# Three moves in a transformer block: a modulation's weights after two steps instead of none, a projection's order, and the first loads' queues

## The chip, the cores and the metric

The kernel runs on one core of one Trainium2 chip. The metric is the device time of one execution in microseconds (us), the median of several runs. A core has five engines that run their own instruction streams: TensorE (PE: matrix products), VectorE (DVE), ScalarE (ACT), GpSimd (POOL) and SyncE (SP, which here only issues transfers). Transfers run on 16 DMA engines, and an instruction stream that issues one goes on to its next instruction, unless the transfer itself must first wait for something: then everything behind it in that stream waits too.

## The reference

A transformer block with adaptive layer norm, all in 32-bit floats: S = 2048 rows, D = 576 columns, 32 heads of 18.

```
mod = (silu(c) @ w_mod).reshape(1, 6, 1, 576)      # c: 1 x 576, w_mod: 576 x 3456
sa, ca, ga, sb, cb, gb = the six of mod
h = layernorm(x) * (1 + ca) + sa
x = x + ga * attention(h, wqkv, wo)                # softmax over 2048 keys, scale 18 ** -0.5
h = layernorm(x) * (1 + cb) + sb
x = x + gb * ((sigmoid(h @ w_gate) * (h @ w_up)) @ w_down)   # inner width 4608
```

## The kernel before

**Start.** The rows of x come in four chunks of 512, each as four tiles of 128 rows (`rows_in`, L421). A chunk is normalized (`normalized`: statistics L215 and L216 on DVE, then the inverse square root from POOL's power L229 and two refinement rounds L232 to L235 on DVE, then L240), turned by PE (`ln_transpose`, L249), scaled by the modulation on ACT into `hT` (with DVE's L268 and L274 for a low-order part), and projected to queries and keys (`project_qk`, L348) and values (L405). `project_qk` makes the query half and the key half one after the other, or with `together` side by side, tile by tile. The first two of the six modulations (1.18 MB per 256 rows of `w_mod`, 2.65 MB in all) are computed here: `load_mod` L125 and matmuls L173. POOL also takes the difference of chunk 0's and chunk 1's keys (`key_differences`, L379 to L384, tiles `kd_d` and `kd_e`), which the maxima use later. In this stage PE, DVE and ACT run in the order in which the code is written, and POOL and SP in an order that a scheduler makes.

**Attention.** 32 units follow, each two heads for 1024 queries, in 16 steps (`kt`) of 128 keys. In a step PE computes scores (L1091), ACT takes their exponentials (L1095), PE multiplies by the values (L676); beside it PE computes scores once more (L571) for a unit ahead, of which DVE takes maxima (L577, L582). When a unit's maxima are complete, L589 on DVE gathers them, and `spread` turns them, splits them (L607 on DVE) and writes them by four transfers (L611, tile `mrows`) into the query tile of the next unit, whose scores L1091 can't be computed before. A unit's end is `outputs`: its sums of exponentials go out to memory and come back turned (L700, L701), DVE takes their reciprocal (L709), which goes out and comes back as a broadcast (L711, L713), POOL multiplies by it (L717). PE, ACT and SP run in the written order here; DVE and POOL in the scheduler's.

**The other four modulations.** In units 1 and 3 `load_mod` (L129 twice with 1.18 MB each, L130 with 0.29 MB) fetches 2.65 MB of `w_mod` each time, `weigh` multiplies them by silu(c) row by row and adds them up on POOL (L143, L146), and in units 2 and 4 `modulate` sums over the partitions on PE (L173), turns the result and hands it out (gates by L204, L205). What the first of these matmuls waits for is the end of `weigh`.

```
if kt == 0 and 0 < u < UNITS - 2:
    load_heads(u + 2)
if u in (1, 3):
    if kt == 0:
        ...
        mods = load_mod(a, b, 1 + u // 2)
        ...
        weighed = weigh(mods)
```

Of the kernel before, what the change touches and what calls it, by code (L numbers as in the profile page):

```python
# [23 lines left out]
P = 128  # L24
S = 2048
D = 576
# [6 lines left out]
DM = 512  # L33
# [52 lines left out]
def tile_block(ctx, tc, x_in, wqkv, wo, w_gate, w_up, w_down, c_in, w_mod, out):  # L86
    nc = tc.nc
    x_rows = x_in[0].rearrange("(t p) d -> p t d", p=P)
# [24 lines left out]
    def bank():  # L113

        turns["bank"] += 1
        return ps[turns["bank"] % 7].tile([P, 512], F32, name=f"s{turns['bank'] % 7}")
# [172 lines left out]
    def terms(wh, wl, cols, tiles=5):  # L289
        got = []  # L290
        for t in range(4):
            got += [(wh[:, t, cols], t), (wh[:, t, cols], 4 + t), (wl[:, t, cols], t)]
        if tiles == 5:
            got += [(wh[:, 4, cols], 8), (wl[:, 4, cols], 8)]
        return got
# [40 lines left out]
    def project_qk(both, ahead=None, together=False):  # L336

        pl = stages[0].tile([P, 2, 1024], F32R, name="pl")
        accs = [bank() for _ in both] if together else []
        all_ = [terms(wh, wl, slice(0, P)) for (_, wh, wl), _ in both]  # L340
        places = [(i, n) for i in range(len(both)) for n in range(len(all_[i]))]
        if together:
            places.sort(key=lambda at: min(at[1] // 3, 4))
        for i, n in places:
            if i == len(accs):
                accs.append(bank())
            (w, t), ch = all_[i][n], both[i][1]
            nc.tensor.matmul(  # L348
                accs[i], w, hT[:, t, ch * 512 : (ch + 1) * 512],
                start=n == 0, stop=n == len(all_[i]) - 1, skip_group_check=together,  # L350
            )
            if n < len(all_[i]) - 1:
                continue
            acc = accs[i]
            if ahead:
                ahead()
            hi, lo = (pl[:, l, i * 512 : (i + 1) * 512] for l in range(2))
            nc.scalar.copy(hi, acc)
            nc.vector.tensor_sub(lo, acc, hi.bitcast(F32))
        for i, ((parts, wh, wl), ch) in enumerate(both):  # L360
            p0 = 0
            for col, n in parts:
                which, f0 = col // D, col % D
                nc.sync.dma_start(
                    (qd, kd)[which][:, f0 : f0 + n, ch * 512 : (ch + 1) * 512]
                    .rearrange("l f n -> f l n").bitcast(F32),
                    pl[p0 : p0 + n, :, i * 512 : (i + 1) * 512].bitcast(F32),
                )
                p0 += n
        return pl  # L370
# [45 lines left out]
    with tc.tile_pool(name="ln", bufs=2) as ln:  # L416
        def rows_in(ch):
            xs = []
            for j in range(4):
                xt = ln.tile([P, 640], F32, name="x", bufs=8)  # L420
                nc.sync.dma_start(xt[:, :D], x_rows[:, ch * 4 + j, :])  # L421
                xs.append(xt)
            return xs

        def normalized(xs, first=None):
            mv = ln.tile([P, 4, 2], F32, name="mv")
            rs = ln.tile([P, 4], F32, name="rs")
            for j, xt in enumerate(xs):
                if first is not None and j == 3:
                    turned_c = po.tile([P, 512], F32, name="o")[:, 0:5]  # L430
                    nc.vector.tensor_mul(first[0:5, 256:384], first[0:5, 0:P], first[0:5, P:256])
                    nc.tensor.transpose(turned_c, first[0:5, 256:384], ident[0:5, 0:5])
                ln_stats(ln, xt[:, :D], mv[:, j, :])
            if first is not None:
                nc.vector.tensor_copy(sc, turned_c)
                nc.vector.tensor_copy(
                    first[:, 384:544].rearrange("p (t c) -> p t c", c=32), sc.unsqueeze(2).to_broadcast([P, 5, 32])
                )
            ln_scales(ln, mv, rs)
            for j, xt in enumerate(xs):  # L440
                ln_apply(xt, xt[:, :D], mv[:, j, 0:1], rs[:, j : j + 1])
            return xs

        order = ExitStack()
        order.enter_context(
            tc.manual_schedule(engines={mybir.EngineType.PE, mybir.EngineType.DVE, mybir.EngineType.Activation})
        )
        wv0 = ExitStack()
        wvp = wv0.enter_context(tc.tile_pool(name="wv0", bufs=1))
        with tc.tile_pool(name="wmp", bufs=1, side="right") as wmp:  # L450
            row = wmp.tile([P, 544], F32, name="mrow")
            nc.vector.memset(row[0:5, 0:P], 0.0)
            nc.scalar.dma_start(row[0:4, 0:P], c_in[0, 0:DM].rearrange("(t p) -> t p", p=P))
            nc.scalar.dma_start(row[4:5, 0:64], c_in[0:1, DM:D])
            rows_now = rows_in(0)
            nc.scalar.activation(row[0:5, P:256], row[0:5, 0:P], AF.Sigmoid)
            warm = early.tile([P, 1], F32, name="warm")
            nc.scalar.activation(warm[0:5], row[0:5, P : P + 1], AF.Exp)
            wm = wmp.tile([P, 5, 2 * D], F32, name="wm")
            wm = load_mod(wm[:, 0:4, :], wm[:, 4, :], 0)  # L460
            zs = normalized(rows_now, row)
            wts, splits = zip(*(load_qk([(o, P)], True) for o in (0, D)))
            rows_now = rows_in(1)
            wv, split_v = load_v(wvp, 0, True)
            turned = []

            def turn_some(*which):
                return lambda: turned.extend(ln_turned(zs, i) for i in which)

            for _ in modulate(  # L470
                row, wm, QUARTERS, [(mcol[:, 1, :], 0.0), (mcol[:, 0, :], 1.0)],
                (turn_some(0, 1), turn_some(2), turn_some(3, 4)),
            ):
                pass
        stages.append(right.enter_context(tc.tile_pool(name="stage", bufs=2, side="right")))
        ones = vaug[:, :, 0 : H * VW].rearrange("p t (h e) -> p t h e", e=VW)
        for t in range(NT):
            nc.gpsimd.memset(ones[:, t, :, DH:VW], 1.0)
        nc.gpsimd.memset(vaug[:, :, H * VW :], 1.0)
        for split in splits:  # L480
            split()
        ln_transpose(ln, None, hT, 0, turned)
        split_v()
        with tc.tile_pool(name="kdp", bufs=1) as kdp:
            zs = normalized(rows_now)
            pls = []
            for ch in range(NCH):
                pls.append(project_qk([(wt, ch) for wt in wts], together=not ch))
                project_v(wv, 0, 4 * ch)
                if not ch:  # L490
                    project_v(wv, 0, 2)
                if ch + 1 < NCH:
                    ln_transpose(ln, zs, hT, (ch + 1) * 512)
                if ch + 2 < NCH:
                    zs = normalized(rows_in(ch + 2))
                if ch:
                    project_v(wv, 0, 4 * ch + 2)
                if ch == 2:
                    key_differences(kdp, pls[0][:, :, 512:1024], pls[1][:, :, 512:1024], 0, P, 0)
        order.close()  # L500
        wv0.close()
# [128 lines left out]
    with tc.tile_pool(name="wv1", bufs=1) as wvp:  # L630
# [3 lines left out]
        for i, parts in enumerate(tiles):  # L634
            wt = load_qk(parts)
# [416 lines left out]
    for u in range(UNITS):  # L1052
        half, p = divmod(u, H // 2)
        qs, ks = heads(u)
        for kt in range(NT):
# [41 lines left out]
            if kt == 0 and 0 < u < UNITS - 2:  # L1097
                load_heads(u + 2)
            if u in (1, 3):
                if kt == 0:  # L1100
                    a = big.tile([P, 8, 640], F32, name="big")
                    a = a.rearrange("p a b -> p (a b)")[:, 0 : 8 * D].rearrange("p (t c) -> p t c", t=4)
                    b = slots.tile([P, 2560], F32, name="w0")[:, 0 : 2 * D]
                    mods = load_mod(a, b, 1 + u // 2)
                    row = slots.tile([P, 2560], F32, name="w1")[:, 0:544]
                    weighed = weigh(mods)
                elif kt >= 5:
                    next(weighed, None)
            elif u in (2, 4) and kt in (2, 4):
                takes = [(ga_b, None), (mcol2[:, 1, :], 0.0)] if u == 2 else [(mcol2[:, 0, :], 1.0), (gb_b, None)]  # L1110
                if kt == 2:
                    weighed = modulate(row, mods[:1], HALVES, takes)
                next(weighed, None)
            if 4 * NT + 8 <= step < FROM0 and step % 4 != 3:
# [541 lines left out]
    for n, (hf, b, k) in enumerate(seq):  # L1656
# [13 lines left out]
        if sevens:  # L1670
# [28 lines left out]
            for v in range(2):  # L1699
# [3 lines left out]
                if v == 0 and f is not None:  # L1703
                    t = gate(st, to)
# [155 lines left out]
```

## Time and profile before

| | us |
|---|---|
| median of 3 runs | 2765.57 (2763.77 to 2766.93) |
| profiled execution | 2765.01 |
| its span, first to last instruction | 2763.2 |
| TensorE busy in the span | 2738.9 |
| start to first exponential of unit 0 | 233.35 |
| first exponential of units 1, 2, 3, 4, 5 | 273.31, 311.25, 350.81, 389.39, 433.38 |

The 1.8 us between the profiled execution and its span lie before the first and after the last instruction. The starts of the units are those of the first L1095 of each; units that run without other work take 37.7 us.

### The profile page before, as it was taken

How to read it: one execution, taken by the hardware profiler on the slowest of the kernel's cores; microseconds unless marked ns; L12 is line 12 of the kernel's file. 1: busy time of each engine (PE TensorE's matmuls, PEld its weight loads, DVE VectorE, ACT ScalarE, POOL GpSimd, SP SyncE). 2: the span in 40 equal slices, each digit the busy share in tenths (PEclk: the TensorE clock that was granted, in tenths of full speed). 3: DMA queues.
4: the chain of work that ended last, by engine and by line, in shares of the span. 5: the costliest groups of instructions: out<-in, count | busy, mean ns of one | idle time of the engine just before them, and what ended most of it. 6: DMA issues, size and time to landing. Idle time of an engine off the chain costs nothing.

```text
span 2763.2 us, 50773 instructions
## 1 busy us (share of the span) xinstructions
PE 2738.9 (99%) x18430; PEld 1829.9 (66%) x18430; DVE 2281.0 (83%) x4318; ACT 1601.7 (58%) x3038; POOL 832.5 (30%) x1077
## 2 busy tenths in 40 slices
PE   7999999999999999999999999999999999999999
PEld 6975444444444544444444888888888888888888
DVE  7278989999999889999883888878888677777777
ACT  4316989999999789999988323333333222222221
POOL 2122327888853213760133222222221100000000
PEclk9999999999999999999999999999999999999999
DMA  5342334555553121432137766667767956666663
GB/s 175 124 156 97 88 105 157 194 189 197 185 172 108 52 57 52 146 100 75 54 116 246 255 234 227 242 224 271 278 244 295 329 198 198 202 195 202 198 198 118
DMA packets 184812, 480.03 MB, mean 174 GB/s; under 512 B 29734, under 2 KB 93742, under 8 KB 174450
## 3 DMA queue, kind: packets, MB, share of 16 engines
q1 hardware_dynamic: 163640, 377.39, 41.1%
q0 software_dynamic: 20912, 99.41, 10.2%
q8 instruction: 145, 2.38, 0.4%
q14 instruction: 105, 0.86, 0.1%
q10 hardware_dynamic: 10, 0.00, 0.0%
HBM read 294.80 MB, written 181.38 MB: 172 GB/s over the span
## 4 chain that ended last, share of the span: by engine, by line
PE 95%; DVE 2%; DMA 1%; issue 1%; SPq 0%; ACT 0%; POOL 0%; DVEq 0%; ACTq 0%; POOLq 0%
PE x L1247 28%; PE o L676 20%; PE s L1091 13%; PE s L571 11%; PE d L1397 8%; PE d L1329 6%; PE s L348 4%; PE s L820 2%; PE s L405 1%; DMA wq_raw<-in_A_wqkv_dram 1%; PE d L1595 0%; DVE Oa L1401 0%; PE s L931 0%; PE s L602 0%; DMA wv_raw<-in_A_wqkv_dram 0%
## 5 line engine op out<-in xcount | busy, mean ns | idle before, releaser
L1095 ACT ACTIVATE p<-s 128x512 f32<-128x512 f32 x2048 | 1070.0, 624 | 88.1 <-PE s L1091 58.5
L577 DVE TENSOR_REDUCE mx<-s 128x1 f32<-128x512 f32 x1568 | 1001.1, 684 | 104.4 <-PE s L571 76.9
L676 PE MATMUL o<-p,vaug 128*32 128x256 f32 (+1 forms) x5848 | 596.3, 478 | 0.2 <-ACT oT L694 0.2
L571 PE MATMUL s<-k,q 54*128 54x512 f32 x1920 | 551.7, 437 | 0.0
L1091 PE MATMUL s<-q,k 56*128 56x512 f32 x1920 | 532.2, 440 | 1.9 <-DMA q<-mrows 1.9
L1091 PEld LDWEIGHTS s<-q,k 56*128 56x128 f32 x1920 | 251.9, 185 | 254.3 <-DVE mx L577 73.7
L571 PEld LDWEIGHTS s<-k,q 54*128 54x128 f32 x1920 | 278.0, 185 | 211.2 <-DVE mx L582 66.2
L1247 PE MATMUL x<-k,w 128*128 128x512 f32 x1512 | 368.0, 391 | 0.0
L1247 PEld LDWEIGHTS x<-k,w 128*128 128x128 f32 x1512 | 277.2, 188 | 53.5 <-issue 1.7
L676 PEld LDWEIGHTS o<-p,vaug 128*32 128x32 f32 x5848 | 116.9, 108 | 206.1 <-issue 189.7
L1397 PE MATMUL d<-wd,hh 128*128 128x288 f32 x1248 | 249.8, 295 | 0.3 <-DVE Oa L1401 0.3
L1247 PE MATMUL x<-w,w 128*128 128x512 f32 x1008 | 244.5, 391 | 0.0
L1247 PE MATMUL x<-big,w 128*128 128x512 f32 x1008 | 244.4, 391 | 0.0
L1247 PEld LDWEIGHTS x<-big,w 128*128 128x128 f32 x1008 | 185.3, 188 | 35.5 <-DVE u L1761 0.2
L1247 PEld LDWEIGHTS x<-w,w 128*128 128x128 f32 x1008 | 184.4, 188 | 33.9
L1397 PEld LDWEIGHTS d<-wd,hh 128*128 128x128 f32 x1248 | 202.1, 188 | 4.3 <-DVE Oa L1401 0.8
L1397 PE MATMUL d<-wd,hl 128*128 128x288 f32 x624 | 184.3, 295 | 0.0
L1401 DVE TENSOR_TENSOR Oa<-Oa,d 128x288 f32<-128x288 f32 x312 | 136.5, 453 | 53.3 <-PE d L1397 49.3
L582 DVE CUSTOM_DVE_ANT_0 over<-s,over 128x512 f32<-128x512 f32 x240 | 163.9, 683 | 1.3 <-PE s L1091 0.3
L580 ACT ACTIVATE over<-s 128x512 f32<-128x512 f32 x240 | 147.6, 615 | 3.1 <-PE s L571 1.1
L1201 POOL TENSOR_TENSOR S<-raw 128x384 f32<-128x384 f32 x72 | 74.5, 1052 | 232.3 <-DVE w L1238 150.1
L1256 ACT ACTIVATE sg<-x 128x512 f32<-128x512 f32 x36 | 21.5, 598 | 205.2 <-PE x L1247 205.2
(273 smaller groups left out, 3807.6 us busy)
## 6 DMA issues: line engine op xcount, KB each, us to landing
ws<-w SPq DMA_DIRECT2D x126, 640.0 KB
w<-ws SPq DMA_DIRECT2D x126, 640.0 KB
wd<-wds SPq DMA_DIRECT2D x19, 1152.0 KB
k<-kd SPq DMA_DIRECT2D x60, 360.0 KB
wds<-w POOLq DMA_DIRECT2D x18, 1152.0 KB, 5.3
wtd<-t POOLq DMA_DIRECT2D x32, 576.0 KB, 4.8
wt<-wtd SPq DMA_DIRECT2D x64, 288.0 KB
wd<-wds SPq DMA_DIRECT2D x52, 288.0 KB
```

The costliest lines, as they stand in the source:

```text
L348: nc.tensor.matmul(accs[i], w, hT[:, t, ch * 512 : (ch + 1) * 512], start=n == 0, stop=n == len(all_[i]) - 1, skip_group_check=together,)
L571: nc.tensor.matmul(sp, qs[rows, qt * P : (qt + 1) * P], ks[rows, at * 512 : (at + 1) * 512], start=True, stop=True,)
L577: nc.vector.tensor_reduce(to, sp, axis=AX.X, op=ALU.max)
L580: nc.scalar.activation(over, sp, AF.Relu)
L582: nc.vector.tensor_tensor_reduce(out=over, in0=sp, in1=over, scale=1.0, scalar=LOWEST, op0=ALU.add, op1=ALU.max, accum_out=mx[:, h * n + q ...
L676: nc.tensor.matmul(acc[32 * j : 32 * j + 32, cols], vaug[:, kt, (2 * p + h) * VW : (2 * p + h) * VW + 32], probs[2 * c + h][:, cols], star ...
L1091: nc.tensor.matmul(sT, ks[rows, kcols], qs[rows, c * 512 : (c + 1) * 512], start=True, stop=True)
L1095: state["exp"] = nc.scalar.activation(pr, sT, AF.Exp, scale=SCALE)
L1247: nc.tensor.matmul(acc[v], w[:, v, a, :], X[s][:, b, :], start=first and n == 0, stop=n == 6, skip_group_check=not first,)
L1329: nc.tensor.matmul(acc, a[:, rows], w[:, k, :], start=n == 0, stop=n == 2)
L1397: nc.tensor.matmul(acc[:, :HALF], a[:, f, rows], w[:, f, cols], start=n == 0, stop=n == 5)
L1401: nc.vector.tensor_add(Oa[:, t, cols], Oa[:, t, cols], acc[:, :HALF])
```

## The change

Three places change. The modulations' weights of units 1 and 3 are requested in step 2 instead of step 0, and the two parts of `modulate` follow in steps 4 and 6 of units 2 and 4 instead of 2 and 4. Chunk 1's queries and keys are projected side by side, as chunk 0's already are. And two of the first four x loads go out from ACT's queue, with the two loads of c moved from there to POOL's.

```diff
@@ -418,7 +418,7 @@
             xs = []
             for j in range(4):
                 xt = ln.tile([P, 640], F32, name="x", bufs=8)
-                nc.sync.dma_start(xt[:, :D], x_rows[:, ch * 4 + j, :])
+                (nc.sync if ch or j % 2 == 0 else nc.scalar).dma_start(xt[:, :D], x_rows[:, ch * 4 + j, :])
                 xs.append(xt)
             return xs
 
@@ -450,8 +450,8 @@
         with tc.tile_pool(name="wmp", bufs=1, side="right") as wmp:
             row = wmp.tile([P, 544], F32, name="mrow")
             nc.vector.memset(row[0:5, 0:P], 0.0)
-            nc.scalar.dma_start(row[0:4, 0:P], c_in[0, 0:DM].rearrange("(t p) -> t p", p=P))
-            nc.scalar.dma_start(row[4:5, 0:64], c_in[0:1, DM:D])
+            nc.gpsimd.dma_start(row[0:4, 0:P], c_in[0, 0:DM].rearrange("(t p) -> t p", p=P))
+            nc.gpsimd.dma_start(row[4:5, 0:64], c_in[0:1, DM:D])
             rows_now = rows_in(0)
             nc.scalar.activation(row[0:5, P:256], row[0:5, 0:P], AF.Sigmoid)
             warm = early.tile([P, 1], F32, name="warm")
@@ -485,7 +485,7 @@
             zs = normalized(rows_now)
             pls = []
             for ch in range(NCH):
-                pls.append(project_qk([(wt, ch) for wt in wts], together=not ch))
+                pls.append(project_qk([(wt, ch) for wt in wts], together=ch < 2))
                 project_v(wv, 0, 4 * ch)
                 if not ch:
                     project_v(wv, 0, 2)
@@ -1097,7 +1097,7 @@
             if kt == 0 and 0 < u < UNITS - 2:
                 load_heads(u + 2)
             if u in (1, 3):
-                if kt == 0:
+                if kt == 2:
                     a = big.tile([P, 8, 640], F32, name="big")
                     a = a.rearrange("p a b -> p (a b)")[:, 0 : 8 * D].rearrange("p (t c) -> p t c", t=4)
                     b = slots.tile([P, 2560], F32, name="w0")[:, 0 : 2 * D]
@@ -1106,9 +1106,9 @@
                     weighed = weigh(mods)
                 elif kt >= 5:
                     next(weighed, None)
-            elif u in (2, 4) and kt in (2, 4):
+            elif u in (2, 4) and kt in (4, 6):
                 takes = [(ga_b, None), (mcol2[:, 1, :], 0.0)] if u == 2 else [(mcol2[:, 0, :], 1.0), (gb_b, None)]
-                if kt == 2:
+                if kt == 4:
                     weighed = modulate(row, mods[:1], HALVES, takes)
                 next(weighed, None)
             if 4 * NT + 8 <= step < FROM0 and step % 4 != 3:
```

What SP's instructions stand like after it, in unit 1 (`-` before, `+` now; L539 and L543 are the last of the heads' loads, `big` and `w` hold the modulation's weights):

```order
 L539 DMA k_2258<-kd 36x1x2560
 L543 DMA k_2258<-kd 18x2560
+L700 DMA osums<-oT 4x512
+L701 DMA sT<-osums 128x16
+L711 DMA osums<-rec 128x16
+L713 DMA R<-osums 128x1x512
 L129 DMA big<-in_w_mod_dram 128x2x1152 x2
-L130 DMA w_2863<-in_w_mod_dram 64x1152
-L700 DMA osums<-oT 4x512
-L701 DMA sT<-osums 128x16
-L711 DMA osums<-rec 128x16
-L713 DMA R<-osums 128x1x512
```

The loads now stand behind all four transfers of the sums, not ahead of them, and L130 follows right behind L129; in unit 3 the same piece reads alike.

On DVE the reciprocal L709 moves among the maxima. In unit 3 it now stands (L577 and L582 are maxima, L589 gathers those of unit 4):

```order
 L577 TENSOR_REDUCE mx_1064<-s_4407 128x1
 L709 RECIPROCAL rec<-sT 128x16
 L589 TENSOR_REDUCE nm<-mx_1064 128x16
 L577 TENSOR_REDUCE mx_1065<-s_4422 128x1
```

and before it stood, 14 rows behind L589 and behind the split L607 of these maxima:

```order
 L607 TENSOR_TENSOR mrows<-s_4512,mrows 16x128
 L577 TENSOR_REDUCE mx_1065<-s_4535 128x1
 L709 RECIPROCAL rec<-sT 128x16
 L577 TENSOR_REDUCE mx_1065<-s_4554 128x1
```

In unit 1 it moves the same way, to this place three maxima ahead of L589 (before, ten rows behind it):

```order
 L577 TENSOR_REDUCE mx_1064<-s_3156 128x1
 L709 RECIPROCAL rec<-sT 128x16
 L577 TENSOR_REDUCE mx_1064<-s_3173 128x1
 L582 ISA over,mx_1064<-s_3180,over 128x512
 L582 ISA mx_1064 128x1
 L577 TENSOR_REDUCE mx_1064<-s_3191 128x1
 L589 TENSOR_REDUCE nm<-mx_1064 128x16
```

On POOL, at the start of the kernel, the key difference L379 changes place with the power L229 of chunk 2's layer norm:

```order
 L243 COPY x<-x 128x64 x4
+L379 TENSOR_TENSOR kd_d<-pl 128x512
 L229 TENSOR_TENSOR r_567<-var,powers 128x4
-L379 TENSOR_TENSOR kd_d<-pl 128x512
 L243 COPY x<-x 128x64 x4
 L380 TENSOR_TENSOR kd_e<-pl 128x512
```

L379 now comes ahead of L229, and what follows L229 keeps its place.

## Rows read from the trace of the kernel before

**Rows 1.** The page: engines' busy time, and one group of instructions (part 5).
```profile
PE 2738.9 (99%) x18430; PEld 1829.9 (66%) x18430; DVE 2281.0 (83%) x4318; ACT 1601.7 (58%) x3038; POOL 832.5 (30%) x1077
...
L1091 PE MATMUL s<-q,k 56*128 56x512 f32 x1920 | 532.2, 440 | 1.9 <-DMA q<-mrows 1.9
```

**Rows 2.** Windows, exponentials alone: length, ACT busy (count), TensorE clock, DMA share, GB/s.
```profile
311.20:348.90 37.70, 32.23 (x62) 1.00 0.21 64
350.80:388.50 37.70, 33.12 (x64) 1.00 0.49 133
389.30:427.00 37.70, 28.56 (x55) 0.91 0.18 54
433.30:471.00 37.70, 33.11 (x64) 1.00 0.56 195
```

**Rows 3.** Timeline of SP's queue, units 1 and 3: start, duration, what is issued.
```profile
276.48 1.37 SPq L129 DMA_DIRECT2D big<-in_w_mod_dram  x2
303.61 0.59 SPq L713 DMA_DIRECT2D R<-osums  x1
...
353.94 1.04 SPq L129 DMA_DIRECT2D big<-in_w_mod_dram  x2
382.94 0.58 SPq L713 DMA_DIRECT2D R<-osums  x1
383.61 2.71 SPq L611 DMA_DIRECT2D q<-mrows  x4
```

**Rows 4.** Timeline of POOL, weighing in units 1 and 3.
```profile
288.14 2.93 POOL L143 TENSOR_SCALAR big<-big,sc 128x576 f32<-128x576 f32 x4 [28.49 <-DMA big<-in_w_mod_dram]
...
303.64 2.80 POOL L146 TENSOR_TENSOR big<-big,w 64x576 f32<-64x576 f32 x2
308.76 1.29 POOL L717 TENSOR_TENSOR R<-oT,R 128x512 f32<-128x512 f32 x1 [2.32 <-ACT p L1095]
...
365.95 2.91 POOL L143 TENSOR_SCALAR big<-big,sc 128x576 f32<-128x576 f32 x4 [21.02 <-PE s L571]
```

**Rows 5.** Timeline of DVE, where the reciprocal stands in units 1 and 3.
```profile
295.67 0.68 DVE L577 TENSOR_REDUCE mx<-s 128x1 f32<-128x512 f32 x1
296.39 0.22 DVE L589 TENSOR_REDUCE nm<-mx 128x16 f32<-128x64 f32 x1
...
373.75 0.22 DVE L589 TENSOR_REDUCE nm<-mx 128x16 f32<-128x64 f32 x1
...
381.24 0.24 DVE L709 RECIPROCAL rec<-sT 128x16 f32<-128x16 f32 x1
```

**Rows 6.** Timeline of TensorE: modulation in unit 2, the second wait in unit 4.
```profile
317.11 0.69 PE L173 MATMUL s<-big,w 128*32 128x288 f32 x8
...
390.25 0.47 PE L1091 MATMUL s<-q,k 56*128 56x512 f32 x1 [0.90 <-DMA q<-mrows]
```

**Rows 7.** Timeline of SP's queue, start of the kernel.
```profile
0.74 1.82 SPq L421 DMA_DIRECT2D x<-in_A_x_dram  x4
```

**Rows 8.** Windows: length, PE, PEld, DVE, ACT, POOL busy, TensorE clock, DMA share, GB/s.
```profile
9.00:12.00 3.00, 3.00 (x30) 1.40 (x28) 1.66 (x9) 0.00 (x0) 1.03 (x1) 1.00 1.06 400
12.00:15.00 3.00, 1.34 (x24) 0.59 (x14) 1.84 (x5) 0.00 (x0) 1.70 (x4) 1.00 1.09 160
15.00:18.00 3.00, 2.87 (x27) 1.81 (x25) 0.83 (x3) 0.17 (x1) 0.00 (x0) 1.00 1.17 274
46.00:50.00 4.00, 3.83 (x10) 3.00 (x11) 3.83 (x13) 0.59 (x1) 0.00 (x0) 0.57 0.06 20
```

**Rows 9.** Timeline of DVE, layer norm of chunk 2.
```profile
51.72 0.17 DVE L234 TENSOR_SCALAR sd<-sd 128x4 f32<-128x4 f32 x1
...
52.52 1.20 DVE L234 TENSOR_SCALAR sd<-sd 128x4 f32<-128x4 f32 x1
```

**Rows 10.** Timeline of POOL, same stretch.
```profile
52.41 1.28 POOL L379 TENSOR_TENSOR kd_d<-pl 128x512 f32<-128x512 f32 x1 [1.12 <-ACT pl L358]
```

**Rows 11.** Timeline of TensorE: the next chunk's transposes.
```profile
56.12 2.08 PE L249 MATMUL s<-ident,x 128*128 128x128 f32 x17 [0.16 <-DVE x L240]
```

## The prediction

> **What bounds the kernel now.** I read the page first. TensorE is busy for 99% of the span [rows 1], so a term counts only where TensorE waits or runs at its lower clock, and both happen in few places. The page puts 1.9 us of waiting on the score matmul L1091, for the row maxima that L611 loads. I then counted softmax exponentials (L1095) in one window per attention unit, each beginning at the unit's first [rows 2]. A unit runs 64 of them in 37.7 us. Unit 2 ends its window with 62: the two modulation matmul groups of its `modulate` cost it 2 x 0.59 us. Unit 4 does the same modulation, and has only 55, at a mean granted clock of 0.91. It also begins late: unit 3's window ends at 388.5 and unit 4's first exponential comes at 389.3. So where unit 3 goes over to unit 4 something is lost beyond modulation: 7 exponentials of 0.59 us are 4.1, and 0.8 of late start make **4.9 us**. The other reading of the same rows agrees: 1.9 us of waiting and 37.7 x 0.09 = 3.4 us of clock make 5.3. Half of TensorE's full clock (1.2 instead of 2.4 GHz) follows the wait.
>
> The SP queue shows why [rows 3]. In unit 1 the loads L129 go out at 276.48, right after the heads' loads, and the softmax sums behind them come late: the broadcast L713 is issued at 303.61. In unit 3 L713 is issued at 382.94 and holds L611 back to 383.61, for maxima that unit 4 needs at 388.
>
> The POOL queue gives the price of weighing [rows 4]: from the first L143 to the end of the last L146 is 303.64 + 2.80 - 288.14 = 18.3 us, back to back. The first L143 starts 11.7 us (288.14 - 276.48) and 12.0 us (365.95 - 353.94) after the loads' issue.
>
> **Modulation weights.** By the code the loads move two steps (4.7 us). By the order they move past L700, L701, L711 and L713, and so must wait on SP for the reciprocal L709 on DVE and for two landings. Where DVE now has L709 decides. In unit 1 it stands three maxima rows ahead of L589, so 3 x 0.68 before 296.39, at 294.4; in unit 3 directly ahead of L589, at 373.75, instead of 381.24 [rows 5]. From L709 to L713 took 382.94 - 381.24 = 1.7 us. So L713 goes out at 296.1 and 375.45, and the loads, which follow it, about 19.6 and 21.5 us later than before.
>
> *Gain at the change from unit 3 to 4.* L611 no longer waits for L713; it follows DVE's L607, some 2.9 us sooner (380.7 for 383.61). The 4.9 us stall goes: **-4.9**. Bounds: 0, if the maxima now lie behind the 2.65 MB of loads on the DMA engines, and -5.3. I take -4.9, since at the 400 GB/s of [rows 8] 2.65 MB take 6.6 us from 376 and are through by 383.
>
> *New wait.* First L143 after L713: nothing stands between but R's broadcast. At best the first tile lands beside R, which took 308.76 - 303.61 = 5.15 us [rows 3, 4]; at worst behind R, with 1.18 MB at 400 GB/s (3.0) more, 8.1. I take 7.1, nearer the upper end because both come from one queue and R is ahead. In unit 1: 296.1 + 7.1 + 18.3 = 321.5. The reader is L173 of `modulate`, which PE reached at 317.11 [rows 6] and now reaches two steps (4.7 us) later, at 321.8. No wait. In unit 3: 375.45 + 7.1 + 18.3 = 400.85. Unit 4 starts at 388.5 without the stall; L173 then stands at 388.5 + (317.11 - 311.20) + 4.7 = 399.1. PE waits 1.75 us, and behind this matmul in PE's hand-written order stand all score matmuls, so nothing fills it. Bounds: 0 at 5.15, 2.75 at 8.1.
>
> *What the clock adds.* The wait of 1.7 us at 14 us (1.34 busy of 3.0) was followed by no drop in the granted clock, 1.00 from 15 to 18; the waits before 46 us were followed by 4 us at 0.57, a loss of 1.7 [rows 8]; unit 4's own stall by 3.4 [rows 2]. Bounds 0 and 3.4, I take 1.7. Unit 4's new cost: 1.75 + 1.7 = **+3.5** (rounded).
>
> The modulation's own matmuls, copies and L204/L205 move by two steps and cost the same. SP's L204/L205 stay behind L713 as before. On POOL L717 of unit 1 now runs ahead of weighing, 1.3 us beside its wait for the loads.
>
> **First rows and c.** SP issues the four x loads in 1.82 us from 0.74 [rows 7], then the modulation weights. Two move to ACT's queue, so the weights start at most 0.91 us sooner. The DMA engines are full from 9 to 12 (400 GB/s), PE idles from 12 to 15 for these weights [rows 8], so most of it arrives: bounds 0 and -0.9, I take **-0.7**. The c loads go from ACT to POOL, behind the building of the identity there; the 1.7 us that PE idles for the weights afterwards cover a c that is later by up to that much.
>
> The Trainium skill (Trainium Kernel Development and Optimization, Key Constraints) says the same in other words, that loads issued from several engines share the 16 DMA engines and save only issue time; by it the gain cannot pass what is saved on SP. No row here has x on two queues.
>
> **Chunk 1's queries and keys side by side.** The same matmuls in another order. PE finishes them earlier, but its next transposes (L249, 56.12) wait for DVE's L240 [rows 11], so the earlier end turns into a longer wait: 0 by itself. What moves the path is POOL: `kd_d` (L379) now stands ahead of chunk 2's L229. Before, it ran from 52.41 to 53.69, and DVE's small L234, on the path to L240, took 1.20 us beside it, where the one before it took 0.17 [rows 9, 10]. That 1.03 us goes, if L379 then runs under the statistics; but L379 now precedes L229, and if its input comes late, L229 waits. Bounds -1.0 and 0.3 (1.28 long, 1.0 gained); I take **-0.7**.
>
> The Trainium skill (SBUF — State Buffer, Who interferes with whom) calls the port pair that DVE and POOL share an exclusive lock, held for a whole instruction. The row agrees: 1.20 of DVE beside 1.28 of POOL. By it the gain is the full 1.0, and the sum 0.3 lower.
>
> **The sum.** -0.7 - 0.7 - 4.9 + 3.5 = -2.8 us. The profiled execution took 2765.01 us, with 2763.2 of span; it would come to 2762.2. The median of the runs is 2765.57, 0.56 above the profiled one; with the same difference I forecast 2762.8. One measurement of this kernel can tell about 0.2% (5.5 us) from no change: the three runs lie within 3.2 us.
>
> **The rivals.**
> A, the forecast: weighing is late in unit 4 alone, 2762.8. Chance 0.45. Its own range is 2760.5 to 2766.1 (at 8.1 us PE waits 0.7 and 2.75, with 1.7 of clock each: -6.3 + 6.85).
> B, the loads land so early that nobody waits. For it: nothing but R is ahead of them, and 5.15 is a row. Against it: R is one transfer of 0.26 MB and has already taken that long. -0.7 - 0.7 - 4.9 = -6.3, 2759.3. Chance 0.33.
> C, the other side: the loads take as long as before. From issue to first L143 they took 11.7 us, behind the heads' loads; against C, these are now long done. Then L143 starts at 296.1 + 0.6 + 11.7 = 308.4 and 387.75, and weighing ends at 326.7 and 406.05: waits of 4.9 and 6.95, with 1.7 of clock each: -6.3 + 15.25 = +9.0, 2774.5. With y us from L713 to the first L143, the waits are y - 7.4 and y - 5.35; with 3.4 of clock the change turns from gain to loss at y = 7.8, and passes 5.5 us at 10.6. Chance 0.09.
> D, the change doesn't remove the stall: L611's maxima land behind the 2.65 MB. Before, the last were there 6.6 us after issue (383.61 to 390.25 [rows 3, 6]); 380.7 + 6.6 = 387.3 is only about half a us before unit 4 wants them. Then -4.9 is missing, PE reaches L173 later by as much and doesn't wait there: -1.4, 2764.2. Chance 0.13.
>
> **How the numbers follow.** Only B is faster by over 0.2%: 0.33. A and D lie within it: 0.58. C is slower: 0.09. The range reaches down to B with its terms at their best (-0.9 - 1.0 - 5.3 = -7.2, 2758.4) and the spread of the runs, 2758.0, and up to A with the clock's upper bound for both waits (-6.3 + 3.45 + 6.8 = +3.95, 2769.5, less the small chance of both), 2768.5; C lies outside.
>
> **What would show it.** Right: in the profile after, no wait for the maxima at 388; the loads issued at 296.7 and 376; L143 first at 303.2 and 382.55; a wait of L173 for POOL in unit 4 and none in unit 2; 64 exponentials in unit 4's window but for modulation and that wait; DVE's L234 at 0.17 in chunk 2. Wrong: L143 before 380.8 in unit 3 (B), after 306 or 385 (towards C); L1091 still waiting for the maxima (D); or an L709 that waits on DVE for the sums' landing and holds L577, which the terms above leave out.

## The result, and the profile after

The changed kernel takes 2772.78 us, median of 10 runs (2769.93 to 2775.45), the one before 2765.45 us over as many (2762.48 to 2767.01): a ratio of 1.0028, 95% interval 1.0018 to 1.0038. It is slower by 7.3 us, where 2.8 us of gain were forecast, and the time lies outside the range. The profiled execution took 2771.52 us, 2769.7 of it the span.

The windows of the exponentials, unit by unit from each first one, as in [rows 2] (units 2, 3 and 4):

```profile
314.30:352.00 37.70, 30.97 (x59) 1.00 0.20 57
356.20:393.90 37.70, 33.15 (x64) 1.00 0.40 119
396.70:434.40 37.70, 29.58 (x56) 0.91 0.24 73
```

Unit 2 has 59 where it had 62; unit 4 has 56 at a clock of 0.91, much as before. The stall that was to go is there, and unit 2 is dearer too. What TensorE waits for, in its own timeline:

```profile
313.86 0.82 PE L1091 MATMUL s<-q,k 56*128 56x512 f32 x2 [0.58 <-DMA q<-mrows]
...
326.47 0.68 PE L173 MATMUL s<-big,w 128*32 128x288 f32 x4 [0.26 <-POOL big L146]
...
396.24 1.12 PE L1091 MATMUL s<-q,k 56*128 56x512 f32 x2 [2.89 <-DMA q<-mrows]
...
410.70 0.69 PE L173 MATMUL s<-big,w 128*32 128x288 f32 x8
```

Twice it waits for the maxima, in units 2 and 4, the second time for 2.89 us where the two waits before came to 1.9 [rows 1]; for the weighing it waits 0.26 us in unit 2 and not at all in unit 4. In windows of all engines (length, PE, PEld, DVE, ACT, POOL busy, granted clock, DMA share, GB/s) that wait looks like this:

```profile
388.00:392.00 4.00, 4.00 (x40) 1.88 (x40) 3.83 (x8) 3.77 (x9) 2.68 (x3) 1.00 1.04 321
392.00:396.00 4.00, 1.35 (x10) 0.19 (x3) 2.07 (x5) 1.90 (x4) 4.00 (x5) 1.00 0.27 84
396.00:400.00 4.00, 3.77 (x20) 1.51 (x24) 1.14 (x2) 2.10 (x4) 4.00 (x5) 0.57 0.36 98
400.00:404.00 4.00, 4.00 (x24) 1.23 (x25) 2.83 (x6) 2.83 (x6) 4.00 (x5) 0.58 0.55 177
```

TensorE is busy for 1.35 of 4 us, and then gets 0.57 and 0.58 of its clock for 8 us. SP's queue shows why the maxima are late, against [rows 3]:

```profile
298.61 0.58 SPq L713 DMA_DIRECT2D R<-osums  x1
299.24 0.98 SPq L129 DMA_DIRECT2D big<-in_w_mod_dram  x2
...
305.45 2.73 SPq L611 DMA_DIRECT2D q<-mrows  x4
...
380.78 0.57 SPq L713 DMA_DIRECT2D R<-osums  x1
381.40 0.98 SPq L129 DMA_DIRECT2D big<-in_w_mod_dram  x2
...
385.53 2.70 SPq L611 DMA_DIRECT2D q<-mrows  x4
389.38 6.62 SPq L724 DMA_DIRECT2D ot<-R  x4
```

The loads go out right behind L713, as the order said, and L611 no longer waits for L713. But 2.65 MB now lie ahead of it: the loads' packets run from 382.55 to 395.02 in the trace's list of transfers, those of the four small L611 from 391.14 to 395.23. On POOL, against [rows 4]:

```profile
308.15 2.92 POOL L143 TENSOR_SCALAR big<-big,sc 128x576 f32<-128x576 f32 x4 [1.65 <-DMA big<-in_w_mod_dram]
...
390.61 2.91 POOL L143 TENSOR_SCALAR big<-big,sc 128x576 f32<-128x576 f32 x4 [1.26 <-PE s L1091]
...
406.01 2.79 POOL L146 TENSOR_TENSOR big<-big,w 64x576 f32<-64x576 f32 x2
```

From L713 to the first L143 it takes 308.15 - 298.61 = 9.5 and 390.61 - 380.78 = 9.8 us. The weighing itself then takes 18.2 us, as before.

At the start of the kernel (against [rows 7]; x from both queues, c from POOL, the sigmoid L456 on ACT, DVE's product L431 that waits for it):

```profile
0.74 0.90 ACTq L421 DMA_DIRECT2D x<-in_A_x_dram  x2
...
1.65 3.57 SPq L125 DMA_DIRECT2D wm<-in_w_mod_dram  x5
2.30 0.54 POOL L454 DMA_DIRECT2D mrow<-in_c_dram  x1
...
9.41 0.31 ACT L456 ACTIVATE mrow<-mrow 5x128 f32<-5x128 f32 x1
...
9.75 0.28 DVE L431 TENSOR_TENSOR mrow<-mrow 5x128 f32<-5x128 f32 x1 [2.19 <-ACT mrow L456]
```

Chunk 2's layer norm on DVE, against [rows 9], and POOL beside it, against [rows 10]:

```profile
52.64 0.17 DVE L234 TENSOR_SCALAR sd<-sd 128x4 f32<-128x4 f32 x1
...
53.44 0.17 DVE L234 TENSOR_SCALAR sd<-sd 128x4 f32<-128x4 f32 x1
```

```profile
49.02 1.29 POOL L379 TENSOR_TENSOR kd_d<-pl 128x512 f32<-128x512 f32 x1 [9.84 <-ACT pl L358]
51.21 1.01 POOL L229 TENSOR_TENSOR r<-var,powers 128x4 f32<-128x4 f32 x1 [0.89 <-DVE var L228]
```

L379 is over before L228 asks for the power, and both L234 take 0.17 us. The transposes behind (L249) start at 54.63, after a wait of 2.6 us for L240, where chunk 1's queries and keys end earlier.

One thing in this profile belongs to the execution, not to the change. In unit 0 TensorE fell to half its clock for 6.8 us. Windows of the kernel before and, below, of the changed one:

```profile
237.00:240.00 3.00, 3.00 (x24) 0.92 (x24) 3.00 (x7) 2.33 (x5) 2.15 (x1) 1.00 0.00 0
240.00:243.00 3.00, 3.00 (x20) 1.35 (x20) 3.00 (x6) 2.55 (x5) 2.89 (x3) 1.00 0.30 77
```

```profile
237.00:240.00 3.00, 3.00 (x14) 0.95 (x14) 1.89 (x4) 0.89 (x3) 2.57 (x2) 0.50 0.03 5
240.00:243.00 3.00, 3.00 (x16) 0.89 (x14) 1.53 (x3) 1.19 (x3) 2.95 (x2) 0.51 0.36 106
```

What TensorE did ahead of it is alike in both, with one wait of 0.93 us for DVE's L359 at 234. The kernel with the start's edits alone (below), whose code is the same up to unit 1, has the wait and no drop. That unit takes 40.0 us in ten of the fourteen profiles of this study, 41.5 in two and 42.9 in two, in kernels of all kinds.

### The profile page after: what moved, and what is told of

The parts are those of the page before. It is cut to its first block, busy times and chain, and to the rows that moved or that the text cites. A ratio compares the mean times of both kernels' runs of the same rounds, so it can differ in the third digit from the quotient of the medians.

```text
span 2769.7 us, 50779 instructions
## 1 busy us (share of the span) xinstructions
PE 2741.3 (99%) x18430; PEld 1831.7 (66%) x18430; DVE 2279.2 (82%) x4318; ACT 1602.0 (58%) x3038; POOL 834.2 (30%) x1079
## 4 chain that ended last, share of the span: by engine, by line
PE 84%; DMA 2%; DVE 2%; issue 1%; SPq 0%; ACT 0%; DVEq 0%; ACTq 0%
PE x L1247 27%; PE o L676 18%; PE s L1091 11%; PE s L571 9%; PE d L1397 8%; PE d L1329 6%; PE s L820 2%; DMA q<-mrows 1%; DMA ws<-w 0%; PE d L1595 0%; DVE Oa L1401 0%; DVE w L1237 0%; PE s L931 0%; DVE mx L577 0%; DVE w L1238 0%
## 5 line engine op out<-in xcount | busy, mean ns | idle before, releaser
L577 DVE TENSOR_REDUCE mx<-s 128x1 f32<-128x512 f32 x1568 | 1000.8, 684 | 109.7 <-PE s L571 78.8
L582 DVE CUSTOM_DVE_ANT_0 over<-s,over 128x512 f32<-128x512 f32 x240 | 163.7, 682 | 1.3 <-PE s L1091 0.3
L580 ACT ACTIVATE over<-s 128x512 f32<-128x512 f32 x240 | 147.9, 616 | 3.7 <-PE s L571 1.8
L1228 ACT CAST w<-S 128x768 fp32r<-128x768 f32 x71 | 59.4, 836 | 138.9 <-POOL S L1201 137.0
```

The costliest lines, as they stand in the source:

```text
L577: nc.vector.tensor_reduce(to, sp, axis=AX.X, op=ALU.max)
L580: nc.scalar.activation(over, sp, AF.Relu)
L582: nc.vector.tensor_tensor_reduce(out=over, in0=sp, in1=over, scale=1.0, scalar=LOWEST, op0=ALU.add, op1=ALU.max, accum_out=mx[:, h * n + q ...
```

## The experiments

All are timed in five rounds beside the kernel before, whose median was 2765.05 us in the first four, 2765.09 in the next four and 2765.39 in the last. A median can move by 1 to 2 us; so the parts are read from the traces, by the length of units 1 to 4 (first exponential to first exponential) and by the first projection matmul.

**The start's edits alone**: everything but the moved modulations.

> The start's three edits (x rows on two queues with c on POOL, chunk 1 side by side) without the moved modulations. In the changed kernel unit 0 begins 0.27 us earlier than before, and then loses 3.0 us in its steps 1 and 2 at half clock, behind the same 0.93 us wait that the kernel before has there without a drop. Theory 1 (the start's edits give -0.3, the drop in unit 0 comes or goes with small shifts in time): 2765.2, or 2768.2 if the drop is there in this run. Theory 2 (all of the +7.3 is the modulations'): 2765.2 and no drop in unit 0. Either way the waits for mrows are those of the kernel before, 1.9 us at the change from unit 3 to 4.

Measured: 2766.46 us, ratio 1.0007 (0.9998 to 1.0016). No drop in unit 0 (40.0 us), units 1 to 4 in 158.2. So the start is not where the 7 us are.

**The moved modulations alone.**

```diff
-                if kt == 0:
+                if kt == 2:
...
-            elif u in (2, 4) and kt in (2, 4):
+            elif u in (2, 4) and kt in (4, 6):
```

> The moved modulations alone, the start as before. Theory 1 (they cost what the changed kernel's trace shows from unit 1 on, 6.37 - 2.73 = 3.6 us): 2769.1, a wait for mrows of about 2.9 us at the change from unit 3 to 4 and one of about 0.6 from 1 to 2, weighing from about 9.5 us behind L713, unit 0 without a half-clock stretch. Theory 2 (all of the +7.3): 2772.8. My prediction for this part was 4.9 - 3.5 = 1.4 us of gain, 2764.1.

Measured: 2772.01 us, 1.0026 (1.0016 to 1.0036). TensorE waits 0.69 us at unit 2's first score matmul (the profile names ACT's L580 for it, and the maxima in the two other kernels with these loads), 1.49 in two parts for the weighing in unit 2, and 3.19 for the maxima of unit 4. By the median theory 2 is right: the modulations account for nearly all of it. Theory 1 came out low because the profile of before, against which I had taken it, has a unit 4 of 44.0 us, with 6.8 us at half clock behind its wait; three others with the old loads have 3.4 us at half clock there, and 41.4 to 42.5.

**x rows and c alone.**

```diff
-                nc.sync.dma_start(xt[:, :D], ...)
+                (nc.sync if ch or j % 2 == 0 else nc.scalar).dma_start(xt[:, :D], ...)
...
-            nc.scalar.dma_start(row[0:4, 0:P], ...)
+            nc.gpsimd.dma_start(row[0:4, 0:P], ...)
```

> x rows on two queues and c on POOL alone. In the changed kernel the first chunk's queries and keys begin 0.95 us later than before, since c arrives late (sigmoid 9.41 instead of 5.57). Theory 1 (this 0.9 stays, as nothing later waits less): 2766.4. Theory 2 (a later wait absorbs it): 2765.5. My prediction for this part was a gain of 0.7, 2764.8. A drop of the clock in unit 0, if it comes, adds 3.

Measured: 2766.09 us, 1.0000 (0.9991 to 1.0009). The sigmoid starts at 9.06 us (9.37 and 9.41 in the other two with c on POOL, 5.47 to 5.82 in the ten profiles with c and x as before). The first projection matmul comes at 21.2, 21.6 and 22.5 us in these three, at 20.1 to 22.5 (mean 20.9) in the ten with the start's loads as before. A loss of about 0.8 us, smaller than the spread of the start.

**The loads one step later instead of two.**

```diff
-                if kt == 0:
+                if kt == 1:
```

> Only the loads of the modulations' weights move, and by one step: on SP they then stand behind L701 but ahead of L711 and L713; modulate stays at steps 2 and 4. Theory 1 (what costs is 2.65 MB on the DMA engines ahead of the maxima; where they run between the sums and the reciprocal they cost nobody): the sums land about 7 us after L700 instead of 14, the loads are through by 298 and 376, the maxima of unit 4 arrive in time, the 4.9 us of the change from unit 3 to 4 go, 2760.6. Theory 2 (any place after the sums is too late for weighing): L173 waits in units 2 and 4, 2765 or more.

Measured: 2767.19 us, 1.0003 (0.9994 to 1.0012). Units 3 and 4 take 37.7 and 39.6 us, 5.3 less than in the profile of before; but unit 2 takes 45.1. Neither theory had that. The timeline there (SP, DVE, POOL, PE together):

```profile
345.37 0.09 DVE L161 MEMSET w<- 128x32 f32 x1 [3.58 <-DMA gates<-w]
...
345.75 3.83 SPq L611 DMA_DIRECT2D q<-mrows  x4
346.11 0.28 PEld L1091 LDWEIGHTS s<-q,k 56*128 56x128 f32 x1 [2.78 <-DVE mx L577]
...
347.28 0.28 DVE L607 TENSOR_TENSOR mrows<-s,mrows 16x128 fp32r<-16x128 f32 x1
```

DVE's fill L161 of the second modulation's row tile, which the scheduler now puts ahead of L607, waits for the first modulation's gates (L204), which still leave the same tile: 3.58 us of idle DVE ahead of it, L607 and the maxima late by as much, and a wait of 2.47 us on PE.

**Side by side alone** (`together=ch < 2`).

> Chunk 1's queries and keys side by side alone. My prediction for it was 0.7 us of gain, all of it from POOL's L379 that no longer runs beside DVE's L234 (0.17 instead of 1.20 us in chunk 2): 2764.4. The rival: the gain on DVE is given back where the next transposes or the next chunk wait, no change, 2765.05. Both are within what the median of runs can tell; the trace shows which by DVE's L234 and by when L240 of chunk 2 and the transposes behind it start, measured from the start of chunk 0's projection.

Measured: 2763.17 us, 0.9993 (0.9984 to 1.0002). From the first projection matmul, chunk 2's first L240 comes after 32.4 us instead of 33.4, and the first exponential of unit 0 after 211.7 instead of 212.7. In the five profiles with this edit that last stretch is 211.5 to 212.1, in the nine without it 212.7 to 212.8. A gain of 1.0 us that lasts.

**The loads at step 1, with a row tile of its own.**

```diff
-                    row = slots.tile([P, 2560], F32, name="w1")[:, 0:544]
+                    if u == 1:
+                        rowt = slots.tile([P, 2560], F32, name="w1")
+                    row = rowt[:, 1024 * (u // 2) : 1024 * (u // 2) + 544]
```

> The loads at step 1 as in the run before, and the second modulation's row tile in another part of the same slot, so that DVE's fill L161 no longer waits for the first one's gates (L204) to be written out. Theory 1 (with the loads between the sums and the reciprocal nothing waits for them; the run before lost its gain to L161 alone): no wait in unit 2, units 3 and 4 of 37.7 and 39.6 us as in that run, so 3.7 to 5.3 us less than before: 2760.5. Theory 2 (the wait in unit 2 comes from the gates themselves or from the maxima's transfer behind L205): unit 2 stays near 45 us and the time at 2767.

Measured: 2762.76 us, 0.9990 (0.9981 to 0.9999). Units 2, 3 and 4 take 39.6, 37.7 and 39.5 us, no wait for the maxima. SP's queue in unit 3:

```profile
362.02 0.35 SPq L701 DMA_DIRECT2D sT<-osums  x1
362.43 0.94 SPq L129 DMA_DIRECT2D big<-in_w_mod_dram  x2
...
374.13 0.34 SPq L711 DMA_DIRECT2D osums<-rec  x1
375.56 0.58 SPq L713 DMA_DIRECT2D R<-osums  x1
380.32 2.71 SPq L611 DMA_DIRECT2D q<-mrows  x4
```

The loads fill the 12 us in which SP has nothing to do but to wait for the reciprocal: their packets run from 363.50 to 373.16, before L711.

**The same with the start's other two edits, c staying on ACT.**

> The same as the run beside it, with two x rows on ACT's queue behind the c loads, which stay on ACT, and chunk 1 side by side. Theory 1 (c late on POOL cost about 2.6 us until the first modulation matmul and 0.95 at the first projection; with c on ACT it is on time): the sigmoid at about 5.6 us, no later first projection than before, and 0.5 to 1.5 us less than the run beside it, 2759.5. Theory 2 (the start is bound by the bytes of x and of the modulation's weights): no difference, 2760.5.

Measured: 2762.18 us, 0.9990 (0.9982 to 0.9999). Theory 1 fell. c is nearly on time (sigmoid at 6.51), but now x is late, since its second row tile stands on ACT behind c and so behind the first of the modulation's weights (SP's and ACT's issues, then DVE's statistics of that tile, which waited 3.91 us):

```profile
1.19 0.42 SPq L125 DMA_DIRECT2D wm<-in_w_mod_dram  x1
...
1.86 0.84 ACTq L421 DMA_DIRECT2D x<-in_A_x_dram  x2
...
8.54 0.82 DVE L215 BATCH_NORM_STATS2 st<-x 128x6 f32<-128x288 f32 x2 [3.91 <-DMA x<-in_A_x_dram]
```

The first projection matmul comes at 22.3 us. c alone on POOL, with x as before, was not run.

**The maxima written from ACT's queue**, with loads at step 2 (and, other than the expectation says, with the second row tile on its own, as in the two runs before).

```diff
-                nc.sync.dma_start(
+                (nc.scalar if state.get("u") in (1, 3) else nc.sync).dma_start(
                     qs[to : to + 1, :]...
```

> The moved modulations alone (loads at step 2, modulate at 4 and 6, row tile as in the second run), with the maxima of units 2 and 4 written from ACT's queue instead of SP's. In the moved version the four small transfers L611 land 10.7 us after their issue, behind 2.65 MB on the same queue. Theory 1 (they wait in line on their own queue): they land 2 to 4 us after issue, the wait for mrows at the change from unit 3 to 4 is 0, units 3 and 4 lose 4 us less than with the loads alone, and ACT pays about 2.7 us of issue twice, some of it on the path: 2768 or less. Theory 2 (the 16 DMA engines themselves are full, whatever the queue): the wait stays at 2 to 3 us and the time at 2772.

Measured: 2776.62 us, 1.0040 (1.0028 to 1.0053). No wait of PE for the maxima. In unit 3 their packets run from 397.36 to 400.84, 4.0 to 7.5 us after the first issue at 393.33, and are in 2.4 us before the loads end (403.25); from SP's queue they ended with the loads, 9.7 us after issue. With nothing ahead (loads at step 1), the first packet comes 1.3 us after issue, the last 3.5, so full engines delay them on another queue too. In unit 1 the other queue gave nothing: the three transfers issued by 306.8 have their packets from 308.47 to 311.6, where on SP's queue in the changed kernel the first 24 of 32 go from 308.57 to 311.9; the loads last until 312.33. So both theories hold in part, and how much is the line on the one queue and how much the full engines isn't settled. The price is on ACT:

```profile
304.62 7.40 ACTq L611 DMA_DIRECT2D q<-mrows  x4
```

Its four issues took 7.40 us in unit 1 (2.72 in unit 3). TensorE waited 6.70 us for ACT's L580 behind them and then ran at half clock, and unit 1 took 49.2 us instead of 37.9.

**Modulate at steps 4 and 6, loads at step 1, own row tile.**

> Loads at step 1, own row, and modulate at steps 4 and 6 as in the changed kernel. Theory 1 (modulate itself costs the same wherever it stands; in the changed kernel units 2 and 4 are dear because of late loads alone): unit 2 at 39.6 us, unit 4 at 39.5, 2762.8 as in the run with modulate at 2 and 4. Theory 2 (at steps 4 and 6 it collides with the unit's own work, 0.5 to 1 us each in units 2 and 4): 2764.3.

Measured: 2762.93 us, 0.9989 (0.9981 to 0.9998). Units 2 and 4 take 39.74 and 39.67 us, 0.15 more than with steps 2 and 4. Theory 1.

**Two fifths of the bytes, loads at step 2, own row tile.**

```diff
-        for t in range(0, 4, 2):
+        for t in range(0, 2, 2):
...
-        nc.sync.dma_start(b[0:64, :], w_mod[DM:D, cols])
```

> The moved modulations (loads at step 2, modulate at 4 and 6, own row), with only the first 256 of the 576 rows of weights loaded and weighed, so 1.18 MB instead of 2.65: the later modulations then lack the other rows. Theory 1 (the number of bytes ahead of the maxima makes them late; 1.18 MB take about 5 to 6 us behind R): the maxima of units 2 and 4 land about 5 us after issue or sooner, no wait of L1091 for them, no wait for weighing, units 2 to 4 at 39.6, 37.7 and 39.5, 2762.8. Theory 2 (not the bytes but the place of the loads or of the reciprocal in the orders): waits as in the run with all bytes, 2770.

Measured: 2760.99 us, 0.9988 (0.9979 to 0.9996). Units 1 to 4 take 37.8, 39.8, 37.7 and 39.7 us. SP's queue in unit 3 (the lines of the code shift by one here: L610 is L611):

```profile
376.75 0.47 SPq L129 DMA_DIRECT2D big<-in_w_mod_dram  x1
380.90 2.75 SPq L610 DMA_DIRECT2D q<-mrows  x4
```

The maxima's last packet lands at 385.27, 4.4 us after issue, and no wait for them or for the weighing is left.

**All bytes, loads at step 2, own row tile.**

> The moved modulations alone with the second row tile apart, all bytes; the counterpart of the run with two fifths of them. Theory 1 (bytes ahead of the maxima): a wait for mrows of about 3 us at the change from unit 3 to 4 with half clock behind it, units 1 to 4 about 6 us above the run with loads at step 1: 2769 to 2772, no better than the moved modulations with the tile of before, where DVE's fill did not wait. Theory 2 (the row tile matters here too): 2767.

Measured: 2771.69 us, 1.0022 (1.0013 to 1.0032), waits for the maxima of 0.45 and 3.25 us in units 2 and 4, 1.2 us for the weighing in unit 2, units 1 to 4 in 164.3. It is also the counterpart of the run with the maxima on ACT, with the same loads. From it to the run with two fifths the edit differs in the bytes alone (and in the weighing of them), and these four units by 9.4 us.

**The best of it: loads at step 1, own row tile, side by side, x and c as before.**

> Loads at step 1, own row, and chunk 1 side by side, with x and c as before: the two edits that the runs showed to help, without the one that did not. Theory 1 (the gains of 2.3 and 1.1 us add up): 2761.7, units 1 to 4 as in the run with the loads at step 1, L240 of chunk 2 1.0 us sooner against chunk 0's projection. Theory 2 (they don't): 2762.8.

Measured: 2762.06 us, 0.9990 (0.9981 to 0.9999), units 1 to 4 in 154.6. By the medians it beats the changed kernel by 10.7 us and the one before by 3.3, barely clear of what can be told. From it to the run without side by side the medians differ by 0.7 us, which doesn't tell the theories apart. The traces speak for theory 1: after the first projection matmul chunk 2's L240 comes 1.1 us sooner (32.35 for 33.44), and units 1 to 4 keep their length.

Units 1 to 4 by where and how much is loaded (us from the first exponential of unit 1 to that of unit 5):

| loads | profiles | units 1 to 4 |
|---|---|---|
| at step 0 (before, start alone, x and c alone, side by side alone) | 4 | 158.2 to 160.1, mean 159.0 |
| at step 2 (changed kernel, modulations alone, the same with own row) | 3 | 163.7 to 164.8, mean 164.3 |
| at step 2, 1.18 MB | 1 | 154.9 |
| at step 1, own row | 4 | 154.5 to 154.8 |

## Why the prediction was wrong

**The step that failed** is "Gain at the change from unit 3 to 4", the -4.9, with the reason that "since at the 400 GB/s of [rows 8] 2.65 MB take 6.6 us from 376 and are through by 383". Nothing of the kind was gained: the stall came back, because the maxima lie behind the loads. Their last packet came 9.7 to 10.2 us after issue in the three profiles with all bytes at step 2, where 3.5 us do with nothing ahead, and TensorE waited 2.89 to 3.25 us. The stall's own price was read rightly: without it, with the loads at step 1, units 3 and 4 take 5.3 us less than in the profile of before (4.3 less than the mean of the four with the old loads). It was rival D that named this mechanism, with 0.13, and it too was priced too low, with a stall no worse than before and none elsewhere. In its place the traces show +5.2 us in units 1 to 4 (164.3 against 159.0): 0.4 in unit 1, 2.6 in unit 2 and 2.2 in units 3 and 4 together.

The size behind the mistake is the rate. 400 GB/s is all that moved from 9 to 12 us, for several tensors. The loads alone took 8.8 to 9.7 us with loads at step 1, and 12.2 to 13.1 at step 2, where R's broadcast runs beside them. In windows over just those packets, in the changed kernel and then with the loads at step 1:

```profile
382.50:395.00 12.50, 10.85 (x91) 4.26 (x83) 11.06 (x22) 11.04 (x23) 5.68 (x7) 1.00 0.83 240
```

```profile
363.50:373.20 9.70, 9.70 (x88) 4.03 (x80) 9.19 (x17) 9.54 (x20) 5.14 (x6) 1.00 0.80 276
```

With 12.5 us from 382.5, the maxima, issued at 385.5, could not be there before 395. With 1.18 MB (the run with two fifths) everything I had forecast for this place did happen, so with the loads at this step the bytes decide it and not the orders. The Trainium skill (DMA: Bandwidth & Descriptors, Queues, rings and completion order) says that SP and ACT each have one ring on each of the same 16 DMA engines, consumed in order on each engine. The trace agrees in unit 3, where the maxima end with the loads on SP's ring and 2.4 us before them on ACT's; in unit 1 it shows no such difference.

**The wait for weighing.** I took 7.1 us from L713 to the first L143, within 5.15 and 8.1; it was 9.5 and 9.8, beyond the upper bound. R itself took 6.6 and 7.3 us from L713 to its reader L717, where I had counted on 5.15, and the first tile of the loads 2.5 to 2.9 more. "PE waits 1.75 us" in unit 4 was wrong in place: there PE was late by the stall and found the sums ready, as D said; in unit 2, where I had none, it waited 0.26 us, and 1.5 and 1.2 in the two runs with the modulations alone. The 1.7 us of clock behind such a wait did not come: none of these was followed by half clock, only the stall of unit 4 was, for 6.8 us. Rival C, the loss, had the right sign, and its 9.0 us are near the 7.3, but its mechanism (both waits for weighing, 4.9 and 6.95 us) was not what happened.

**What I left out** is that the same line forms at the change from unit 1 to 2 (waits of 0.45 to 0.69 us) and that unit 2 then loses 2.3 to 2.9 us. In the changed kernel 1.1 of that is the late weighing (steps 4 to 7 took 12.2 us, against 11.1 for steps 2 to 5 before), 0.6 the wait for the maxima in its first step, and 0.7 its last two steps, for which I have no cause. In the two runs with the modulations alone the late weighing makes 2.1 to 2.4 (13.2 and 13.5 us) and the first step 0.6, and the last two steps cost nothing.

**The reciprocal's place** was read rightly: L709 came directly ahead of L589 in unit 3 and three maxima ahead in unit 1, L713 1.7 us behind it. The modulation's move by two steps costs 0.15 us a unit, near the nothing that I gave it.

**x rows and c**: -0.7 forecast, +0.8 measured, in the noise of the start. The sentence that failed is that the idle time for the weights covers a later c. The weights did start 0.95 us sooner (1.65 for 2.60), but c from POOL held the sigmoid back by 3.8 us, more than the 1.7 that I allowed, and DVE, where the fourth row tile's statistics stand behind L431, with it.

**Side by side**: -0.7 forecast, -1.0 measured, by the mechanism named: POOL's L379 out of L234's way. The full 1.0 that the rule of the Trainium skill gave (SBUF — State Buffer, Who interferes with whom) was nearer than my value; L234 with 0.17 on both rounds agrees with it.

**The sum** as the runs give it: +5.2, +0.8 and -1.0 are 5.0. The medians put the modulations at 6.3 to 7.0 and the whole at 7.3; some 2 us of it I can't place, though the intervals of the two runs with the modulations alone (4.4 to 10.0 and 3.6 to 8.8 us) hold 5.2. Likewise the loads at step 1 give 4.3 us in units 1 to 4, and 2.3 to 2.5 in the medians. Part of such rests are the drops of the clock in unit 0 (1.5 or 3 us, in 4 of 14 profiles) and units 10 to 16, which take 264.3 to 264.6 us in six profiles and 264.9 to 266.1 in the eight in which TensorE waits there as well: 0.2 to 0.6 us for ACT's L694 in unit 10, or 0.2 to 0.9 for the maxima from unit 14 to 15.

## What to carry to other kernels

Before a load is moved, list the small transfers that are issued behind it on the same queue until it is through, and price it by its own first and last packet elsewhere in the trace, not by the total rate of a busy stretch. Here a large load cost nothing where its queue idled, waiting for another engine (between the sums and their reciprocal), and one step decided between 4 us gained and 5 lost. When a tile's allocation moves, look at what a scheduler does with the instructions that fill it: a 0.09 us fill ahead of the maxima cost 5.5 us.

## What the runs showed that I had not expected

- Small issues waited for the large loads to land: SP's four L724 took 6.62 us in unit 3 and 5.35 in unit 1 of the changed kernel, 1.37 before, and ended at 396.0, a us after the loads. In the trace each transfer takes over the semaphore (the counter that tells of a landing) of an earlier one, and first waits for that one; for the last three L724 these were the loads themselves (4.7 us for the two L129, 0.7 for L130 in unit 3). In the same way ACT's fourth L611 waited in unit 1 for the landing of its own first (311.37, issue at 311.39), which makes its 7.40 us.
- c, two loads of 2.3 KB together, let ACT begin 5.3 us after POOL's last issue (2.84 to 8.12) against 2.5 after ACT's (1.82 to 4.28).
- The same matmuls with the same 0.93 us wait are followed by half clock in one execution and by full clock in another.
